# Block 0 of the long filter: folding moved from VectorE into TensorE's accumulation, with a mirrored copy by ScalarE, another order and other buffers for w2

## The chip, the cores and the metric

The kernel runs on one core of one Trainium2 chip. The metric is device time of one execution in microseconds (us). Three runs before the change gave 187.36 to 187.61, median 187.47. A time is compared within the same chip; lower is better.

## The reference

Two branches share the input `q` (2048 rows S, 640 channels D, bf16), and a gate mixes them:

```
x = A_q
g = sigmoid((x * gate_w).sum(-1))                       # one number per row
# branch A: a long convolution over the 2048 rows, per channel
kv = (4-tap causal filter of k) * v
y  = irfft(rfft(pad(kv)) * rfft(pad(ssm_k)))[:2048]     # length 4096
a  = x * (y + kv * ssm_D)
# branch B: an MLP across the rows
h = layernorm(x);  u = gelu(einsum("sd,sf->df", h, w1) + b1)      # F = 1536
b = (einsum("df,fs->ds", u, w2) + b2).T
out = g * a + (1 - g) * b
```

`ssm_k` is the long filter: 640 channels, each with 2048 taps. `ssm_D` enters the kernel as an extra added to tap 0 (row `drow`).

## The kernel before

**The long convolution** is cut into P = 4 blocks of n = 512 rows. Filter block i and signal block j are each turned into frequency space by matmuls with sine and cosine tables (`TFc`, `TFs` for the filter, `AFc`, `AFs` for the signal), multiplied pairwise (`pair`), and turned back (`inverse`). A block is folded first: sample and mirrored sample are added and subtracted, so that the transform needs half as many products. For filter block i this is `w_turn`:

- `wnat{i}` [128, 5 x 512]: the block as it lies in memory, with channels on the partitions (five groups of 128 channels), taps along the free axis. `wnat_load` brings it in one DMA of 640 KB.
- `en{..}`: the folded block. Two VectorE operations over 128 x 1280 add and subtract forward and backward views; four small ones (five columns each, one for each channel group) set the samples that have no mirror image.
- The folded block has to have taps on the partitions. For blocks 0 and 1 TensorE transposes it, 20 matmuls of 128 columns against an identity (`ident`, printed as `idp`) into four PSUM tiles of 640 columns. Blocks 2 and 3 go through a DMA transpose.
- `WEV` says which engine copies each of the four tiles to `eo{i}`: for block 0 ScalarE, VectorE, ScalarE, VectorE; for block 1 four times ScalarE.
- For block 0 the fourth tile also takes `drow`, by two matmuls with one row of the identity.

`w_freq` (tag `wf{i}`) then runs the transform on `eo{i}`, eight tiles of 640 columns in matmuls of 320, evicted by ScalarE to `W{i}` or, for block 1, `Wo`. In the rows of the profile `TFs#2`, `TFc#0` and the like name one of these tiles.

**What else runs in the first 50 us.** ScalarE makes the tables (`Sin`, `Abs`: `TFs`, `adx`, `TFc`, `AFs`, `AFc`) from `idx`, which VectorE makes from `frow`, which GpSimd makes. VectorE takes layer-norm statistics of the 16 row tiles of `q` (`stats`, `mv`) and normalises them to `h`. `shd` and `dg` prepare the 4-tap filter; `cv0`, `cv1` run it on TensorE as 64 x 64 matmuls of `dg` and `kT`, and ScalarE evicts to `ks`. The rows of `v` come partly by plain DMA, partly by GpSimd's indirect gather (`rev` holds the indices). `es0`, `es1` are the folded signal blocks, and TensorE's first MLP matmuls (`m1_0`, on `h` and `w1`) fill in between.

**The second MLP layer** (`mlp2`, tag `m2_q`) takes `w2` in eight pieces of 256 columns, 768 KB each, through three buffers `w2_0`, `w2_1`, `w2_2`; the turn of buffers is (0, 1, 0, 1, 2, 0, 1, 2). A piece is loaded by SP's queue when the buffer's last reader is done. The inverse transforms, the gate (`gg`, `omg`, `c2`) and the products with `q` (`xe`) close the kernel. The very last operations on VectorE are two `fin` operations (scalar_tensor_tensor from PSUM) after the last piece of w2, followed by two stores.

**What sets the order.** Each operation is first gathered in `_Plan` with its engine, reads and writes. `ORDER`, a list of all operation numbers written into the file, says in which sequence they are emitted; each engine works through its own queue in that sequence, and a tracker puts in the semaphore waits. DMAs stand in the queue of SP (plain ones) or GpSimd (gathers, adds to memory), so a DMA that waits for a buffer holds those behind it. PSUM is four tiles `pp` of 128 x 1024 f32, given out in turn, each free again when its eviction is done. Buffers in SBUF lie at written-out offsets (`OFFS`) and share space when their lifetimes are apart; `v1`, for one, lies over `wnat0`.

All matmuls carry line 311 in the profile, ScalarE's activations 695, VectorE's tensor_tensor 657, tensor_scalar 664, copies 672, plain DMAs 265 (262 on GpSimd), gathers 726, the evictions by VectorE 1023.

Of the kernel before, what the change touches and what calls it, by code (L numbers as in the profile page):

```python
# [422 lines left out]
def _checked(items, offs, base, top):  # L423
# [49 lines left out]
def _build(nc, A_q, A_k, A_v, A_shift_k, A_ssm_k, A_ssm_D, B_x, B_w1, B_b1, B_w2, B_b2, gate_w, out):  # L473
# [5 lines left out]
    n = S // P  # L479
# [990 lines left out]
```

## Time and profile before

| | |
|---|---|
| median of three runs | 187.47 us (187.36 to 187.61) |
| the profiled execution | 188.28 us |
| its span, first to last instruction | 186.4 us |
| TensorE busy | 176.8 us (95%), 1578 matmuls |
| VectorE busy | 178.8 us (96%), 252 instructions |
| ScalarE busy | 127.1 us (68%), 205 instructions |
| GpSimd busy | 35.3 us (19%), 68 instructions |
| DMA traffic | 40.37 MB, mean 217 GB/s |

Times in the profile count from the start of the span; 1.88 us of the profiled execution lie outside it. A row of the timeline has start, duration (both us), engine, line, operation, output<-input, shape, and in brackets the idle time of the engine before it and who ended that. A row of the groups has the number of instructions behind an x, then busy us, the mean of one in ns, and the idle time before them. In the table of stretches each engine has its busy time and, behind an x, its instructions, in the order PE, PEld (weight load), DVE (VectorE), ACT (ScalarE), POOL (GpSimd), then granted TensorE clock, busy share of the DMA engines and GB/s. The granted clock is 1.00 throughout.

### The profile page before, as it was taken

The page shows a single profiled execution, that of the slowest core. Times are in us where ns is not written, and L with a number is a line of the kernel's source. Part 1 is how long each engine was busy: PE and PEld are TensorE (multiplying, and loading weights), DVE is VectorE, ACT ScalarE, POOL GpSimd, SP SyncE. Part 2 cuts the span into 40 slices and gives each one's busy share as a digit, 9 for nine tenths or more (in the row PEclk, how much of TensorE's full clock was granted, in tenths as well). Part 3 has the DMA queues.
Part 4 walks back from the last instruction along what each step waited for, and adds up shares of the span by engine and source line. Part 5 has one row for each costly group of instructions (what it writes and reads, how often), then busy time and mean ns, then how long its engine had stood idle before and what let it go on. Part 6 is the DMA issues. An engine that isn't in the chain of part 4 may idle for free.

```text
span 186.4 us, 3923 instructions
## 1 busy us (share of the span) xinstructions
PE 176.8 (95%) x1578; PEld 122.0 (65%) x1578; DVE 178.8 (96%) x252; ACT 127.1 (68%) x205; POOL 35.3 (19%) x68
## 2 busy tenths in 40 slices
PE   7778899999999999999999999999999999999992
PEld 2255667566667766777777777677776777777771
DVE  7999999999999999999899999999999999999784
ACT  3979899879499579638830146644889555875870
POOL 8367067610000000011000000000000500350262
PEclk9999999999999999999999999999999999999999
DMA  5999999798995998598769999988999998999394
GB/s 148 344 311 242 168 184 232 212 212 211 240 333 120 221 234 195 117 224 219 161 143 175 270 252 211 216 156 263 282 270 294 281 190 242 320 182 234 72 136 146
DMA packets 80448, 40.37 MB, mean 217 GB/s; under 512 B 39400, under 2 KB 80238, under 8 KB 80430
## 3 DMA queue, kind: packets, MB, share of 16 engines
q1 hardware_dynamic: 77694, 37.18, 80.9%
q0 software_dynamic: 2736, 2.95, 10.2%
q8 instruction: 12, 0.20, 0.5%
q14 instruction: 6, 0.05, 0.1%
HBM read 26.03 MB, written 7.54 MB: 180 GB/s over the span
## 4 chain that ended last, share of the span: by engine, by line
PE 64%; DVE 23%; DMA 6%; issue 2%; POOL 2%; ACT 1%; DVEq 0%; POOLq 0%
PE pp L311 64%; DVE stats L931 6%; DMA w<-in_B_w_dram 6%; DVE v L657 3%; DVE en L657 3%; DVE es L657 2%; DVE idx L664 2%; DVE W L657 2%; POOL rstd L936 1%; DVE h L665 1%; DVE eo L1023 1%; DVE mv L933 1%; DVE A L657 1%; DVE xe L657 1%; DVE dg L1012 1%
## 5 line engine op out<-in xcount | busy, mean ns | idle before, releaser
L311 PE MATMUL pp<-h,w 128*128 128x320 bf16 x384 | 56.6, 299 | 0.2
L311 PE MATMUL pp<-gT,w 128*128 128x320 bf16 x336 | 48.7, 299 | 0.6 <-DMA w<-in_B_w_dram 0.5
L311 PEld LDWEIGHTS pp<-h,w 128*128 128x128 bf16 x384 | 36.8, 98 | 15.9 <-issue 1.6
L311 PEld LDWEIGHTS pp<-gT,w 128*128 128x128 bf16 x336 | 32.5, 98 | 13.9 <-DMA w<-in_B_w_dram 1.1
L657 DVE TENSOR_TENSOR tt<-A,W 128x3840 bf16<-128x3840 bf16 (+2 forms) x16 | 27.8, 1738 | 0.2
L695 ACT ACTIVATE A<-pp 128x640 bf16<-128x640 f32 x32 | 21.3, 703 | 8.1 <-PE pp L311 8.1
L657 DVE TENSOR_TENSOR Z<-Z,tt 128x3840 bf16<-128x3840 bf16 (+1 forms) x14 | 26.1, 1867 | 0.1
L262 POOL DMA_DIRECT2D out_dram<-xe x3 | 4.1, 1367 | 66.4 <-DVE y L657 57.5
L695 ACT ACTIVATE pq<-pp 128x640 bf16<-128x640 f32 x16 | 11.0, 703 | 7.2 <-PE pp L311 7.1
L695 ACT ACTIVATE gT<-pp,bf 128x640 bf16<-128x640 f32 x12 | 9.5, 791 | 7.9 <-PE pp L311 7.9
L695 ACT ACTIVATE o<-pp,c,omg 128x640 bf16<-128x640 f32 x13 | 11.5, 881 | 4.6 <-PE pp L311 4.6
L931 DVE BATCH_NORM_STATS2 stats<-x 128x6 f32<-128x320 bf16 x32 | 13.7, 473 | 0.0
L695 ACT ACTIVATE xe<-xe,gg 128x640 bf16<-128x640 bf16 x16 | 12.8, 827 | 0.9 <-DMA xe<-rows_q 0.8
L695 ACT ACTIVATE ks<-pp 128x512 bf16<-128x512 f32 (+1 forms) x24 | 11.3, 523 | 3.1 <-PE pp L311 3.1
L657 DVE TENSOR_TENSOR Z<-A,W 128x3840 bf16<-128x3840 bf16 x6 | 12.8, 2153 | 0.5 <-PE pp L311 0.5
L695 ACT ACTIVATE W<-pp 128x640 bf16<-128x640 f32 x18 | 12.1, 720 | 1.5 <-PE pp L311 1.5
L675 POOL MEMSET W<- 1x640 bf16 x4 | 2.7, 665 | 51.1 <-ACT nq L695 49.8
L657 DVE TENSOR_TENSOR W<-W 128x2560 bf16<-128x2560 bf16 x8 | 11.9, 1486 | 0.2
L311 PE MATMUL pp<-kT,dg 64*64 64x256 bf16 x320 | 10.2, 270 | 0.3 <-ACT Wo L695 0.3
L657 DVE TENSOR_TENSOR Z<-Z 128x1280 bf16<-128x1280 bf16 (+1 forms) x16 | 10.0, 653 | 0.1
L311 PE MATMUL pp<-eo,TFc 128*128 128x320 bf16 x48 | 8.9, 300 | 1.2 <-ACT TFc L695 1.2
L262 POOL DMA_DIRECT2D out_dram<-rows_o x6 | 7.0, 1355 | 15.3 <-DMA out_dram<-o 13.2
(156 smaller groups left out, 305.1 us busy)
## 6 DMA issues: line engine op xcount, KB each, us to landing
w<-in_B_w_dram SPq DMA_DIRECT2D x24, 256.0 KB, 4.5
w<-in_B_w_dram SPq DMA_DIRECT2D x8, 768.0 KB, 6.2
wnat<-in_A_ssm_k_dram SPq DMA_DIRECT2D x4, 640.0 KB, 5.2
x<-in_A_q_dram SPq DMA_DIRECT2D x7, 320.0 KB, 6.5
out_dram<-o SPq DMA_DIRECT2D x6, 320.0 KB, 5.4
v<-in_A_v_dram SPq DMA_DIRECT2D x4, 320.0 KB, 3.9
rows_q<-in_A_q_dram SPq DMA_DIRECT2D x8, 160.0 KB, 3.5
xe<-rows_q SPq DMA_DIRECT2D x8, 160.0 KB, 6.1
```

Source lines behind the costliest of these rows:

```text
L262: ins = engobj.dma_start(out_ap, in_ap, accum_op=ALU.add)
L311: ins = self.nc.tensor.matmul(ps_ap, lhsT=lhsT, rhs=rhs, start=start, stop=stop)
L657: return vop(eng, c, lambda e: e.tensor_tensor(out_, in0, in1, op), [in0, in1], [out_], pr, kind="tt")
L664: return e.tensor_scalar(out_, in0, s1, None, op0=op0)
L665: return e.tensor_scalar(out_, in0, s1, s2, op0=op0, op1=op1)
L675: return vop(eng, 0.03 + nel(ap) / 1200.0, lambda e: e.memset(ap, val), [], [ap], pr, kind="ms")
L695: return e.activation(out_, src, func, **kw)
L931: vop("DVE", 0.393, (lambda o_, i_: lambda e: e.bn_stats(o_, i_))(o_, i_), [i_], [o_], pr, kind="bn")
L933: vop("DVE", 0.11, (lambda o_, i_: lambda e: e.bn_aggr(o_, i_))(o_, i_), [i_], [o_], pr, kind="ba")
L936: vop("POOL", 0.7, (lambda o_, i_, e_: lambda e: e.tensor_tensor(o_, i_, e_, ALU.pow))(b["rstd"][:, sl], b["vpe"][:, sl], bc(c_mh, [[8, 12 ...
L1012: vop("DVE", 1.45, lambda e: e.tensor_tensor(o_, ib, sb, ALU.mult), [i_, s_ap], [o_], 1.8, kind="tt")
L1023: vop("DVE", 0.74, lambda e: e.tensor_copy(dst, src()), [src], [dst], 0.3, ps=[p_], kind="ev")
```

## The change

For block 0 alone (`PF = (0,)`) `w_turn` calls a new function, `pf_turn`.

- `wnat0` comes in two DMAs of 320 KB, first and second half of the taps, each half of a channel group stored 257 elements apart (`GAP`) so that one free column stands behind every half.
- Five small VectorE operations (five or ten columns) form `sd0` and write the samples that have no mirror image into `wnat0` itself, so that every forward and backward run of 128 columns is regular.
- One ScalarE copy, `wr`, writes both mirrored halves (128 x 1280) backwards.
- TensorE folds: for each 128 columns one matmul with `wnat0` against `ident` and one with `wr` against `ident` or against its negative (`idn`) are accumulated in the same PSUM place. 40 matmuls of 128 columns in place of 20. `drow` is added with `two`, a row holding 2, and the evictions scale partition 0 by a half (`cst` column 7).
- The six `en` operations of block 0 and the memset of `wnat0`'s margin go. GpSimd gets two more memsets of `cst`, two of `two`, and the making of `idn`.
- The w2 pieces take buffers in the turn (0, 1, 0, 2, 1, 0, 2, 1).
- `ORDER` is another list. In it the first operations stand as before (VectorE's up to its 22nd, ScalarE's up to its third `Abs`). ScalarE then runs `AFs`, the table `TFc` and block 1's evictions in another mixture, `wr` after the third `Wo` eviction of block 1, and block 0's two evictions spread among the remaining `Wo`. TensorE runs block 1's transposes, six of its eight transform tiles, then block 0's transposing groups, the one with `drow` first, with transform tiles between them, and one group behind the three tiles of `cv0`. GpSimd's first gather of `v0` stands right behind the last memset of `TFs`; the gathers of `v1` stand later. In SP's queue the `v0` load stands before the first transpose to `kt0`; piece 3 and piece 4 of w2 are asked for in the new turn, and two loads of `v2` stand behind piece 2's.

```diff
+    PF = (0,)
...
+        buf("idn", [128, 128], BF16, 0, 30)
+        buf("wr", [128, 2, DC, 128], BF16, 0, 30)
+        buf("two", [1, 128], BF16, 0, 30)
+        for i in PF:
+            buf(f"sd{i}", [128, 2, DC], F32, 0, 30)
...
+        memset(cst[:, 7:8], 1.0, 0.2)
+        memset(cst[0:1, 7:8], 0.5, 0.2)
+        memset(b["two"][:, :], 0.0, 0.3)
+        memset(b["two"][:, 0:1], 2.0, 0.3)
...
+        ts(b["idn"][:, :], b["id_i"][:, :], 0.0, -1.0, ALU.is_equal, ALU.mult, 0.25, eng="POOL")
...
+        GAP = n // 2 + 1
+        RT = DC * GAP
+        def pf_turn(i):
+            plan.tag = f"wt{i}"
+            wn = b[f"wnat{i}"]
+            eo = b[f"eo{i % 2}"]
+            for hf in range(2):
+                dst = bass.AP(tensor=wn, offset=hf * RT, ap=[[DC * n + 16, 128], [GAP, DC], [1, n // 2]])
+                dma(dst, dram(A_ssm_k, i * n + hf * (n // 2), [[S, 128], [128 * S, DC], [1, n // 2]]), f"wnat{i}_{hf}", -300.0)
+            pr = 1.0 + 0.1 * i
+            def at(v, extra=None):
+                return bass.AP(tensor=wn, offset=v, ap=[[DC * n + 16, 128]] + (extra or []) + [[GAP, DC]])
+            sd = b[f"sd{i}"]
+            tt(sd[:, 0, :], at(RT + 128), at(128), ALU.subtract, pr)
+            tt(sd[:, 1, :], at(RT + 128), at(128), ALU.add, pr)
+            tt(at(GAP - 1), at(RT), sd[:, 0, :], ALU.subtract, pr)
+            tt(at(RT + GAP - 1), sd[:, 1, :], at(0), ALU.subtract, pr)
+            io = at(RT, [[-RT, 2]])
+            tt(io, io, sd[:, :, :], ALU.add, pr)
+            wr = b["wr"]
+            act(wr[:, :, :, :], bass.AP(tensor=wn, offset=GAP - 1, ap=[[DC * n + 16, 128], [RT, 2], [GAP, DC], [-1, 128]]), ACT.Copy, pr)
+            for e in range(2):
+                for k in range(2):
+                    p_ = _PS()
+                    xd = i == 0 and e == 1 and k == 1
+                    mms = []
+                    for c in range(DC):
+                        f0 = c * GAP + (0 if k else RT)
+                        fw = bass.AP(tensor=wn, offset=f0, ap=[[DC * n + 16, 128], [1, 128]])
+                        bw = wr[:, k, c, :]
+                        mms.append((p_, c * 128, 128, fw, ident, not xd or c in (0, 4), False))
+                        mms.append((p_, c * 128, 128, bw, b["idn"][:, :] if e else ident, False, not xd))
+                    if xd:
+                        mms += [(p_, c0, cn, b["two"][:, :], b["drow"][:, c0:c0 + cn], False, True)
+                                for c0, cn in ((0, 512), (512, 128))]
+                    pe([p_], mms, pr, cost=0.56 + (0.35 if xd else 0.0))
+                    evict(WEV[i][2 * e + k], eo[:, e, k, :], p_, cst[:, 7:8])
...
         def w_turn(i):
+            if i in PF:
+                return pf_turn(i)
...
-            nm = f"w2_{(0, 1, 0, 1, 2, 0, 1, 2)[q]}"
+            nm = f"w2_{(0, 1, 0, 2, 1, 0, 2, 1)[q]}"
...
```

`evict` takes the scale as a new argument: on ScalarE as the activation's scale, on VectorE as a tensor_scalar multiplication in place of the plain copy. The new list of `ORDER` is left out above.

More of the change, by code (lines that the diff above doesn't have):

```diff
@@ L1016, in _build @@
         WEV = (("ACT", "DVE", "ACT", "DVE"), ("ACT", "ACT", "ACT", "ACT"))
-        def evict(eng, dst, p_):
-            if eng == "ACT":
+        GAP = n // 2 + 1
[35 more added lines that the diff above has]
+                    evict(WEV[i][2 * e + k], eo[:, e, k, :], p_, cst[:, 7:8])
@@ L1020, in evict @@
+        def evict(eng, dst, p_, sc=None):
+            if sc is not None and eng == "ACT":
+                act(dst, flat(p_), ACT.Copy, 0.3, scale=sc, ps=[p_])
+            elif sc is not None:
+                src = flat(p_)
+                vop("DVE", 0.74, lambda e: e.tensor_scalar(dst, src(), sc, None, op0=ALU.mult), [src, sc], [dst], 0.3, ps=[p_], kind="ev")
+            elif eng == "ACT":
                 act(dst, flat(p_), ACT.Copy, 0.3, ps=[p_])
@@ L1237, in mlp2 @@
             w2_load(q)
-            w2 = b[f"w2_{(0, 1, 0, 1, 2, 0, 1, 2)[q]}"]
+            w2 = b[f"w2_{(0, 1, 0, 2, 1, 0, 2, 1)[q]}"]
             o_ = b[f"o{(q // 2) % NO}"]
```

75 rows, old and new, of tables (OFFS, ORDER) are left out of this document.

## The prediction

> **What bounds the kernel now.** I read the page's head and its chain first, then the busy time of each engine in stretches, then the chain in order of time, then the instructions of the first 50 us.
>
> ```profile
> span 186.4 us, 3923 instructions
> PE 176.8 (95%) x1578; PEld 122.0 (65%) x1578; DVE 178.8 (96%) x252; ACT 127.1 (68%) x205; POOL 35.3 (19%) x68
> PE 64%; DVE 23%; DMA 6%; issue 2%; POOL 2%; ACT 1%; DVEq 0%; POOLq 0%
> ```
>
> TensorE and VectorE are both full over the span, so the question is which of them binds where. The stretches below (us, then PE, PEld, DVE, ACT and POOL busy) are cut at the first depthwise-convolution matmul of block 0 (20.47), at the last wait for VectorE (49.76) and at the one wait for a w2 piece (143.57).
>
> ```profile
> 8.24:20.47 12.23, 9.61 (x86) 6.21 (x87) 12.23 (x38) 10.66 (x19) 6.58 (x8) 1.00 1.15 281
> 20.47:49.76 29.29, 28.56 (x323) 19.04 (x324) 29.16 (x70) 25.27 (x45) 10.26 (x13) 1.00 0.94 202
> 49.76:143.57 93.81, 93.23 (x867) 66.73 (x867) 92.74 (x76) 59.89 (x103) 1.24 (x2) 1.00 0.92 218
> 143.57:182.90 39.33, 39.31 (x288) 27.98 (x288) 37.06 (x50) 25.88 (x34) 11.54 (x11) 1.00 0.91 207
> ```
>
> TensorE is idle for 12.23 - 9.61 = 2.62 us in the first stretch, 0.73 in the second, 0.58 in the third, 0.02 in the last. From 20.47 on TensorE is the bound almost everywhere; VectorE shapes only the first 50 us. So the change is paid in TensorE time and can gain only what it takes out of these 3.95 us, plus a little at the tail.
>
> ```profile
> 1.05 0.15 POOL cst L675 x4
> 1.25 0.60 POOL frow L797 x2
> 1.87 2.21 DVE idx L664 x4
> ...
> 12.66 1.48 DVE en L657 x2
> ...
> 14.27 0.09 DVE en L672
> 14.36 0.15 DVE en L657 x2
> ...
> 15.89 0.09 DVE en L672
> ...
> 17.67 0.72 DVE eo L1023
> ...
> 49.76 67.37 PE pp L311 x644
> ...
> 133.21 10.31 DMA w<-in_B_w_dram
> 143.57 36.61 PE pp L311 x268
> ```
>
> These pieces of the chain (start, us, what) hold what the change touches: block 0's fold on VectorE, its two evictions there, and the load of w2 that TensorE waits for.
>
> **VectorE, part by part.** Six `en` operations of block 0 go: 1.48 + 0.09 + 0.15 + 0.09 = 1.81 us. Five five-column operations on `sd0` and `wnat0` come; at 0.15 / 2 = 0.075 each that is 0.38. They depend on one another, but statistics of LN stand between most of them, which hides the latency; with that cover gone each would cost its full duration, some 0.1 more. The two evictions stay and get a scale operand; a plain one takes 0.72 here and I keep that. VectorE comes out 1.4 us ahead, minus 0.1: two more GpSimd memsets stand ahead of the second `frow` (0.15 / 4 = 0.04 each), which releases `idx` and with it the whole start.
>
> **TensorE.** Block 0's transposes go from 20 to 40 matmuls of 128 columns.
>
> ```profile
> 12.05 0.99 PE L311 MATMUL pp<-eo,TFc 128*128 128x320 bf16 x6 [1.18 <-ACT TFc L695]
> 14.51 0.71 PE L311 MATMUL pp<-eo,TFc 128*128 128x320 bf16 x4
> 15.66 0.44 PE L311 MATMUL pp<-idp,en 128*128 128x128 bf16 x5
> 16.03 0.44 PE L311 MATMUL pp<-drow,idp 1*128 1x512 bf16 x2
> 18.45 0.73 PE L311 MATMUL pp<-idp,en 128*128 128x128 bf16 x10 [0.52 <-DVE eo L1023]
> 19.70 0.45 PE L311 MATMUL pp<-idp,en 128*128 128x128 bf16 x5 [0.52 <-ACT eo L695]
> 20.47 0.74 PE L311 MATMUL pp<-kT,dg 64*64 64x256 bf16 x20 [0.32 <-ACT Wo L695]
> ```
>
> Five take 0.44 and ten 0.73, so one more costs (0.73 - 0.44) / 5 = 0.058, each with its own weights; twenty cost 1.1 us. A 320-column matmul takes (0.71 - 0.30) / 3 = 0.137, 0.30 being the drain of a last one. [...]
>
> **ScalarE**, which decides when these matmuls can run:
>
> ```profile
> 8.73 1.99 ACT L695 ACTIVATE eo<-pp 128x640 bf16<-128x640 f32 x3
> 11.26 0.73 ACT L695 ACTIVATE TFc<-adx,cst 128x512 bf16<-128x512 f32 x1
> 11.88 0.73 ACT L695 ACTIVATE AFs<-idx,cst 128x512 bf16<-128x512 int32 x1
> 13.62 3.09 ACT L695 ACTIVATE Wo<-pp 128x640 bf16<-128x640 f32 x5 [1.01 <-PE pp L311]
> ```
> ```profile
> L695 ACT ACTIVATE W<-pp 128x640 bf16<-128x640 f32 x18 | 12.1, 720 | 1.5 <-PE pp L311 1.5
> L695 ACT ACTIVATE W<-pp,cst 128x640 bf16<-128x640 f32 x6 | 4.8, 800 | 0.2 <-PE pp L311 0.2
> L695 ACT ACTIVATE w2r<-w 128x1536 bf16<-128x1536 bf16 x2 | 3.0, 1478 | 0.0
> ```
>
> A back-to-back eviction steps 0.60 ((3.09 - 0.70) / 4), a table 0.62 (11.88 - 11.26). The new backward copy `wr` has 1280 columns; the nearest row is `w2r`, also read backwards, 1478 ns for 1536, so 1478 x 1280 / 1536 = 1.23 us. It cannot be below the 0.72 of a 640-column eviction nor above 1.48. Two evictions gain a scale operand: 0.08 each.
>
> The new order, walked with these steps. ScalarE from 8.73: AFs, `eo1`, TFc, three more `eo1`: 8.73 + 0.62 + 0.60 + 0.62 + 0.60 + 0.60 + 0.70 = 12.5, then `Wo` from 12.7, `shd`, two more `Wo`, and `wr` from 14.6 to 15.8. VectorE, which starts on `sd0` a little before its old 12.66, has prepared `wnat0` by about 14.1, ahead of ScalarE. TensorE begins block 1's transform some 1.2 later than before, but its 1.18 wait for TFc goes; the 28 matmuls that stand ahead of block 0 (28 x 0.137 = 3.8) are covered by ScalarE's steps, and block 0 begins when `wr` is there, at 15.8 + 0.2 = 16.0. Then come 10 small and the two `drow` ones (0.95), 10 small (0.55), 12 and 8 of 320 (1.6 and 1.1), 10 small (0.55): 20.8, when the convolution's first PSUM tile is free. By then it has done ten small and eight 320-column matmuls more than before at 20.47: 0.56 + 1.10 = 1.66 us of work for 0.38 of time. That is 1.28 won by shorter waits, against 1.1 that is added: **0.1 to 0.2 us net in the first stretch**. Bounds: 1.1 lost when no wait shrinks, 2.62 - 1.1 = 1.5 won when all go.
>
> Second stretch. The last ten folded matmuls come after the convolution and end at about 23.9; VectorE's copy of them, its 77th operation, then runs 24.0 to 24.8, and the next transform of block 0 waits 0.7 for it (new). LN's normalisations, queued behind that copy, stay ahead of TensorE's need in my walk. Two short waits of the size of the 0.32 before the convolution come for `es0` and for the Gelu table. So up to some 44 us I get no gain. After that VectorE's lead shows:
>
> ```profile
> PE pp L311 <- DMA w<-in_B_w_dram: 0.5, 1, 0.5
> PE pp L311 <- DVE v L657: 0.3, 1, 0.3
> ```
>
> The wait for `v` at 49.76 and two smaller gaps before it close: **0.4 us**, between 0.73 and a loss of 1.3 (both new waits on the path with nothing won for them).
>
> Third stretch. The wait for w2 piece 3:
>
> ```profile
> 131.44 4.57 SPq L265 DMA_DIRECT2D w<-in_B_w_dram  x2
> 143.57 1.26 PE L311 MATMUL pp<-gT,w 128*128 128x320 bf16 x8 [0.46 <-DMA w<-in_B_w_dram]
> ```
>
> Piece 3 went to buffer 1, which piece 1 leaves only at 133.2, and landed 10.3 us later, behind the `xe` loads and piece 4. Now it goes to buffer 2, free long before, and piece 4 takes buffer 1; TensorE asks for that after piece 2 (48 matmuls, 6.6), 16 of `af3` (2.2), 24 of piece 3 (3.3) and two more: over 12 us against 10.3. **0.5 us won**, between 0 and 0.6. SP's queue moves too: two loads of `v2` now stand behind piece 2's wait for buffer 0, which can hold VectorE up by half a us near 132, where TensorE needs `es2` only at 138.
>
> **The loads and GpSimd.** `wnat0` comes in two pieces with 512-byte runs instead of 1024, and the first gather of `v0` moves forward to about 8.3, right behind the last TFs memset.
>
> ```profile
> DMA packets 606, 0.68 MB, mean 356 GB/s; under 512 B 63, under 2 KB 606, under 8 KB 606
> DMA packets 1274, 0.69 MB, mean 301 GB/s; under 512 B 14, under 2 KB 1273, under 8 KB 1273
> 12.77 2.51 POOL L726 DMA_INDIRECT v<-in_A_v_dram,rev  x1 [0.20 <-issue]
> ```
>
> The first row is the stretch 9.6 to 11.5, in which the old `wnat0` landed, the second 139 to 141.3, where 512-byte runs of w2 came in. For 640 KB (0.655 MB) that is 1.84 and 2.18 us: 0.3 later, and VectorE, busy with statistics, asks for it at about 12.4, so I count nothing. With that cover gone it costs 0.3, and up to 1.0 if the gather's 320 KB (half of the first time, 0.9) goes ahead of it as well. [...]
>
> **Tail.**
>
> ```profile
> 183.14 1.01 DVE L1358 SCALAR_TENSOR_TENSOR xe<-pp,omg,xe 128x320 bf16<-128x320 f32 x2
> ```
>
> These last two operations start 0.26 after TensorE's end (182.90 less rounding); in the new order the addition of `c2` before them stands earlier, so up to 0.15 goes: **0.1**.
>
> **The sum.** First stretch -0.1, second -0.4, w2 -0.5, start +0.1, tail -0.1: -1.0 us. The span of 186.4 becomes 185.4, the profiled execution's 188.28 becomes 187.3 (1.9 lie outside the span and stay), and the median of 187.47, 0.8 under that execution, becomes **186.5**. The ends of the terms: -1.5 to +1.1, -0.73 to +1.3, -0.6 to 0, 0 to +0.3, -0.15 to 0. All at their ends together is unlikely, since they trade: what is won early makes the later waits longer.
>
> **Rivals.**
>
> *The ring of ScalarE, VectorE and TensorE slips.* ScalarE is busy 10.66 of 12.23 in the first stretch and 25.27 of 29.29 in the second, and `wr` adds 1.2 there. The last folded group, VectorE's copy of it and the next transform of block 0 hang on one another. If ScalarE's steps come 1 us or more later than I summed, no early wait shrinks and the 1.1 of matmuls is paid in full, and 0.3 of the new 0.7 wait: +1.1 + 0.3 - 0.5 + 0.1 = +1.0, **188.5**, slower. It speaks for it that ScalarE's ladder has 1.3 us of slack at most; against it that the six evictions ahead of `wr` need only 0.60 each while 28 matmuls run beside them. Chance 0.31.
>
> *Late `wnat0`.* The 0.3 of the load shows and eats VectorE's lead: -1.0 + 0.3 + 0.4 = -0.3, **187.2**. For it: the gather beside it; against it: 0.5 us of cover. That the other turn of buffers does not do its work, because another load holds piece 4 back, comes to about the same (-1.0 + 0.5 = -0.5, 187.0). Chance 0.14 together.
>
> *VectorE's lead is passed on whole.* The first stretch gives 0.7, the second its 0.7, w2 0.6, start +0.1: -1.9, **185.6**. The 0.52 waits for `eo` and 0.5 for `v` speak for it, the 1.1 of added matmuls against it. Chance 0.10.
>
> **How the numbers follow.** The forecast has 0.45. Its own ends are some 0.5 to either side (the terms' uncertainties, mostly the first stretch's 0.4 and the second's 0.3): 186.0 to 187.1. The 80% range reaches to 185.5 for the third rival and 188.6 for the first. This kernel's runs lie 0.25 apart, and 0.2%, or 0.37 us, is about what can be told from no change: faster is under 187.10, slower over 187.84. Faster takes the forecast, the third rival and nothing of the first: 0.55; same most of the second and the forecast's upper end: 0.14; slower 0.31.
>
> **What the profile after would show.** Right: TensorE busy about 178 (1.16 more), its idle time before 20.5 under 1.5 us, first folded group at about 16.0, `wr` at 1.2 us; the small matmuls' rows at 0.058 a piece; no wait for `w` near 143; the wait for `v` near 49 gone. Wrong: `wr` later than 16.5 or over 1.5 us; a wait over 1 us before a transform of block 0 in the second stretch; a new wait of TensorE on a w2 piece after 145; VectorE idle on `wnat0` before 14.

## The result and the profile after

The changed kernel took 190.04 us in the median of six runs (189.10 to 191.24), the kernel before 187.67 (187.36 to 188.03): a ratio of 1.0109 (95% interval 1.0076 to 1.0142). Six more runs (changed_again, below) gave 1.0145 (1.0108 to 1.0182). Ratios here and below are those on record; they differ a little from the quotient of the two medians (1.0126 here). Medians and ranges take in every run, the ratios leave out the slow ones, over 1.5% above the fastest run of their kernel (one each of w2turn_alone, changed_w1_early, fold_early_warm11 and the kernel before). The prediction was 186.5, in a range up to 188.6: wrong in sign, and the range too narrow.

The profiled execution took 189.92, its span is 188.1. The head of its page, and the shares of its chain by engine and by line:

```profile
span 188.1 us, 3967 instructions
PE 177.5 (94%) x1598; PEld 122.8 (65%) x1598; DVE 177.2 (94%) x251; ACT 128.7 (68%) x206; POOL 34.5 (18%) x72
PE 66%; DVE 12%; ACT 10%; DMA 7%; issue 2%; POOL 1%; POOLq 1%; SPq 0%; DVEq 0%
PE pp L311 66%; DMA w<-in_B_w_dram 4%; DMA wnat<-in_A_ssm_k_dram 4%; ACT W L702 3%; DVE stats L943 3%; DVE en L664 2%; DVE idx L671 2%; ACT h L702 2%; ACT ks L702 1%; DVE v L664 1%; ACT pq L702 1%; ACT A L702 1%; DVE y L664 1%; POOL out_dram L739 1%; DVE dg L1024 1%
```

VectorE's share of the chain has fallen from 23% to 12%: in its place stand ScalarE (10%, before 1%) and two transfers, of w1 and of `wnat2`. (Lines have moved: 702 is what 695 was, 664 what 657 was.) TensorE's rows that begin with a wait, the first row of the convolution (21.16) and the last row of all, from its timeline (start, duration, then idle time and releaser in brackets):

```profile
8.38 0.92 PE L311 MATMUL pp<-idp,en 128*128 128x128 bf16 x10 [1.76 <-DVE en L664]
10.19 0.45 PE L311 MATMUL pp<-idp,en 128*128 128x128 bf16 x5 [0.28 <-ACT eo L702]
11.48 1.30 PE L311 MATMUL pp<-eo,TFs 128*128 128x320 bf16 x8 [0.84 <-ACT eo L702]
16.20 0.22 PE L311 MATMUL pp<-idp,wnat 128*128 128x128 bf16 x1 [0.55 <-DVE dg L1024]
21.16 2.40 PE L311 MATMUL pp<-kT,dg 64*64 64x256 bf16 x80
25.29 0.43 PE L311 MATMUL pp<-eo,TFc 128*128 128x320 bf16 x2 [0.53 <-DVE eo L1076]
36.02 0.30 PE L311 MATMUL pp<-es,AFc 128*128 128x320 bf16 x1 [0.40 <-ACT ks L702]
44.86 0.45 PE L311 MATMUL pp<-h,w 128*128 128x320 bf16 x2 [0.55 <-DMA w<-in_B_w_dram]
45.47 0.43 PE L311 MATMUL pp<-v,AFs 128*128 128x320 bf16 x2 [0.16 <-DVE AFs L672]
115.80 1.26 PE L311 MATMUL pp<-h,w 128*128 128x320 bf16 x8 [0.55 <-DMA w<-in_B_w_dram]
182.60 1.79 PE L311 MATMUL pp<-gT,w 128*128 128x320 bf16 x12
```

The account in TensorE's time: the first real matmul 0.14 later (8.38 for 8.24), 1.1 for twenty more matmuls, and waits of 3.86 from there on. Before, the waits behind 8.24 were 1.18, 0.52, 0.52, 0.32, 0.19, 0.29 and 0.46, together 3.48. So 0.14 + 1.1 + 0.38 = 1.6; TensorE's last row ended at 182.88 and now ends at 182.60 + 1.79 = 184.39, which is 1.5. The last 0.2 of the span's 1.7 is the tail. The early waits did shrink, from 2.54 to 1.67 up to the convolution; what they gave came back as waits for `eo` and `ks`, which the prediction had foreseen, and for two pieces of **w1**, which it had not looked at. This one profile accounts for 1.7 us; the medians lie 2.4 apart.

The row at 16.20 needs care. Its releaser is printed as `dg`, which ended at 16.06, 0.14 before it. But in changed_again (below) `dg` ended at 16.11 and this matmul came only at 17.37. What both profiles share is `wr`: the matmul starts 0.26 us after its end (15.94 and 17.11), and the six further kernels below in this order with the new fold show 0.25 to 0.29. So `wr` released it; `dg` happened to end in between.

The second profile of the changed kernel (label changed_again, span 189.2) shows one thing more. Stretches as in the prediction's table, first of the one profile, then of the other:

```profile
8.40:11.50 3.10, 1.97 (x25) 1.36 (x26) 3.10 (x12) 3.10 (x6) 1.36 (x3) 1.00 1.15 323
11.50:13.60 2.10, 2.10 (x15) 1.16 (x16) 2.06 (x10) 1.81 (x5) 0.00 (x0) 1.00 1.19 335
```
```profile
8.40:11.50 3.10, 1.99 (x25) 1.38 (x26) 3.10 (x12) 3.10 (x6) 1.42 (x3) 1.00 1.16 321
11.50:13.60 2.10, 2.10 (x9) 1.24 (x10) 2.07 (x10) 1.02 (x2) 0.00 (x0) 0.54 1.10 370
13.60:16.20 2.60, 2.60 (x16) 1.65 (x14) 2.60 (x9) 2.33 (x5) 0.72 (x1) 0.71 1.27 233
```

After the same thin stretch (TensorE busy 2.0 of 3.1 us) the granted clock fell to 0.54: nine matmuls in 2.1 us instead of fifteen. Block 0's first folded matmul then came at 17.4 instead of 16.2. The clock is not the whole of the loss, as far as it is listed: of the changed kernel's twelve runs the five with a clock of 0.997 or more took 189.10 to 191.24, all of them above the kernel before.

### The profile page after: what moved, and what is told of

It is laid out like the page before. It is cut to its first block, busy times and chain, and to the rows that moved or that the text cites. A ratio compares the mean times of both kernels' runs of the same rounds, so it can differ in the third digit from the quotient of the medians.

```text
span 188.1 us, 3967 instructions
## 1 busy us (share of the span) xinstructions
PE 177.5 (94%) x1598; PEld 122.8 (65%) x1598; DVE 177.2 (94%) x251; ACT 128.7 (68%) x206; POOL 34.5 (18%) x72
## 4 chain that ended last, share of the span: by engine, by line
PE 66%; DVE 12%; ACT 10%; DMA 7%; issue 2%; POOL 1%; POOLq 1%; SPq 0%; DVEq 0%
PE pp L311 66%; DMA w<-in_B_w_dram 4%; DMA wnat<-in_A_ssm_k_dram 4%; ACT W L702 3%; DVE stats L943 3%; DVE en L664 2%; DVE idx L671 2%; ACT h L702 2%; ACT ks L702 1%; DVE v L664 1%; ACT pq L702 1%; ACT A L702 1%; DVE y L664 1%; POOL out_dram L739 1%; DVE dg L1024 1%
## 5 line engine op out<-in xcount | busy, mean ns | idle before, releaser
L311 PE MATMUL pp<-h,w 128*128 128x320 bf16 x384 | 58.1, 299 | 1.1 <-DMA w<-in_B_w_dram 1.1
L702 ACT ACTIVATE pq<-pp 128x640 bf16<-128x640 f32 x16 | 10.7, 709 | 6.2 <-PE pp L311 6.2
L311 PEld LDWEIGHTS pp<-kT,dg 64*64 64x64 bf16 x320 | 8.2, 105 | 2.0 <-issue 1.3
L311 PE MATMUL pp<-eo,TFs 128*128 128x320 bf16 x48 | 8.2, 299 | 0.8 <-ACT eo L702 0.8
```

The costliest lines, as they stand in the source:

```text
L311: ins = self.nc.tensor.matmul(ps_ap, lhsT=lhsT, rhs=rhs, start=start, stop=stop)
L702: return e.activation(out_, src, func, **kw)
```

## The experiments

Two explanations stood against each other from the start: the fold itself, and the order written with it. Later a third was added, the clock. Each kernel was timed against the kernel before on the same chip; ratios are to that, with 95% intervals. The groups of experiments ran on different chips (median of the kernel before: 188.22, 188.18, 188.63, 188.47 and 188.47), so kernels of different groups are compared by their ratios.

**changed_again.** No edit.

> The changed kernel once more, for a second profile and for its scatter (its six runs lay between 189.10 and 191.24, the kernel before between 187.36 and 188.03). Theory R (the new order's transfers): the time that comes back is in waits for w1 pieces, near 44 us and near 115 us, and they differ from run to run, so the gaps before m1_1 and m1_5 differ between the two profiles by more than 0.3 us while the first 25 us agree within 0.1. Theory F (the fold itself): the loss is in matmuls added (1.1 us) and in the wait for block 0's last eviction near 25 us, equal in both profiles; then the scatter must have another origin.

190.65 (190.26 to 192.41). The waits for w1 are there again, 1.4 together instead of 1.1, but each differs by less than the 0.3 that theory R asked for, and the first 25 us did not agree, since the clock fell. Neither theory had that.

**order_alone, fold_alone, w2turn_alone** take the change apart.

```diff
 order_alone = before
-ORDER (old)                      +ORDER (new), old fold's operations in the new ones' places
-w2 turn (0,1,0,1,2,0,1,2)        +(0,1,0,2,1,0,2,1)
 fold_alone = after
-ORDER (new)                      +ORDER (old), wr ahead of the first Wo, v1's gathers behind block 0's matmuls
-w2 turn (0,1,0,2,1,0,2,1)        +(0,1,0,1,2,0,1,2)
 w2turn_alone = before
-w2 turn (0,1,0,1,2,0,1,2)        +(0,1,0,2,1,0,2,1), loads of pieces 3 and 4 change places
```

> The new order and the new turn of w2 buffers with the old fold of block 0 on VectorE (its six operations where the five new ones stand, 20 transposing matmuls, no wr, none of the added memsets). Theory R: the waits for w1 near 44 and 115 us (0.55 each in the changed kernel's profile) are there without the new fold; VectorE runs 1.4 us behind, so dg and the fold are late near 16 us. I expect 188.0 to 189.0, that is slower than before by 0.5 to 1.3. Theory F: without the 1.1 us of matmuls and the wr copy the new order is no worse than the old one and keeps the gain at w2: 187.0 to 187.5.

> The new fold of block 0 (five small operations, wr, 40 matmuls, scaled evictions, added memsets) in the old order with the old turn of w2 buffers; wr stands ahead of ScalarE's first Wo, the gathers of v1 behind block 0's last matmuls, which read what they overwrite. Theory F: +1.1 of matmuls, +0.15 at the start, the two waits of 0.52 before block 0's small groups remain, so 188.7 to 189.5. Theory R: the matmuls lie partly in those waits, which the old order has anyway, and no w1 wait is new: 187.7 to 188.4.

> The kernel before with only the new turn of w2 buffers; pieces 3 and 4 change places in SP's queue, so piece 3 is loaded where piece 4 was (131.4 us). Both theories: TensorE's wait of 0.46 for w2 at 143.6 goes, 187.0 to 187.2 (-0.5). If the time is taken back by later loads or by the tail, 187.4 to 187.6.

- order_alone: 189.46, ratio **1.0075** (1.0051 to 1.0099).
- fold_alone: 188.01, ratio **0.9993** (0.9974 to 1.0011).
- w2turn_alone: 189.05, ratio **1.0046** (1.0024 to 1.0068).

In the old order the fold makes no difference to the median, and the new order costs without it. Theory F fell in both places; theory R's range held fold_alone, and order_alone lies a little above its range. This does not close the sum: order_alone at 1.0075 stands against 1.0145 for the changed kernel on the same chip (intervals apart) and 1.0109 in its first six runs, so 0.3 to 0.7% come from having both at once. Nor did order_alone show theory R's mechanism. The only profile of it is of its slowest run (191.59); there the clock was 0.50 from 11.5 to 16.2 us, and of TensorE's waits for loads one of 0.72 was for piece 2 of w2 at 136.8, two of 0.20 for w1 at 34.8 and 46.2, and none near 115. TensorE's waits in fold_alone:

```profile
PE pp L311 <- DVE en L664: 1.9, 1, 1.9
PE pp L311 <- ACT TFc L702: 1.2, 1, 1.2
PE pp L311 <- DVE wz L682: 1.1, 1, 1.1
PE pp L311 <- ACT Wo L702: 0.8, 1, 0.8
PE pp L311 <- ACT eo L702: 0.3, 1, 0.3
PE pp L311 <- DVE v L664: 0.3, 1, 0.3
```

No wait for `es`, `w` or VectorE's `eo` is left in it. Its convolution began 1.1 us later than before (21.60 for 20.47), just the added matmuls; two thirds of a microsecond of that was left at 50 us, 0.5 at 133, and nothing after 143. The first half vanished in waits that stood behind it. The rest did not: TensorE wanted piece 3 of w2 at 143.4, 0.3 later than before, and it had landed at 142.5, 1.05 earlier than before, though it was asked for 0.6 later; it took 8.6 us and not 10.3. Why, no run shows. The runs say the same in another way: eight of fold_alone's twelve lie at 188.00 to 188.02, while the kernel before scatters from 187.37 to 189.02 on that chip. Its best runs are 0.6 faster than any of fold_alone; the medians do not differ beyond the interval.

w2turn_alone was the surprise. In its profile the wait of 0.46 for piece 3 is gone, and one of 0.6 stands at 142.9 for piece 4: in the old order TensorE asks for piece 4 *before* piece 3, and piece 4 now has the buffer that comes free at 133. The turn alone moves the wait to another piece. That and a wait of 0.3 for w1 near 107 stand against the forecast gain of 0.5; both theories missed here. In the new order, where the wait at 143 did go, the turn was not priced by itself.

**changed_w1_early, changed_warm20** try the two suspects in the changed kernel. (`NWARM` is the number of warming matmuls: 512 columns each on a constant tile `wz`, results unused, with which TensorE fills the time until its first real work.)

```diff
 changed_w1_early: SP's queue
+w1_2 first half (m1_1), w1_1 second half (m1_5) earlier
 kt0 transpose (36.0) ; v1 ;
-w1_2 first half
 ...  w1_1 first half (100.7) ; [second half now here] ; v2 ; v2 ; xt (gt1) ; w2 piece 1
-w1_1 second half (108.6)
 changed_warm20
-    NWARM = 15
+    NWARM = 20
```

> The changed kernel with two loads moved in SP's queue: the first half of w1 for m1_1 (w1_2, asked for at 40.7 us behind the transposing kt0 load and v1) goes ahead of that kt0 load, and the second half of w1 for m1_5 (w1_1, asked for behind piece 1 of w2 at 108.6) goes right behind the first half at 100.7. Theory R (late w1 loads of the new order): TensorE's waits of 0.55 to 0.8 near 44.9 and 115.8 us go, and the median falls by 0.9 to 1.3, to about +0.5 to +0.9% over the kernel before. Theory C (a lower granted clock in the first 20 us): the scatter stays and the median falls by less than 0.5.

> The changed kernel with 20 warming matmuls instead of 15, which reach to about 7.7 us and shorten TensorE's pause before block 1's transposes from 1.8 us to about 0.8. Theory C: the pause makes the granted clock fall between 11.5 and 17 us in some executions (0.991 over the span in the second profile); with the shorter pause every run shows a clock of 0.995 or more and the median falls by 0.3 to 0.8. Theory R: nothing changes (within 0.2), because ScalarE's steps set those microseconds and the lost time lies later.

changed_w1_early: 190.33, ratio 1.0094 (1.0063 to 1.0125), in two groups: four of its runs at 188.27 to 188.96 (clock 0.998 to 1.0), eight at 190.15 to 191.83 (six of them with a clock of 0.980 to 0.991). The profile is of the best run; TensorE's waits in it:

```profile
PE pp L311 <- ACT eo L702: 1.1, 2, 0.8
PE pp L311 <- DVE wz L682: 1.1, 1, 1.1
PE pp L311 <- DVE dg L1024: 0.5, 1, 0.5
PE pp L311 <- DVE eo L1076: 0.5, 1, 0.5
PE pp L311 <- DVE es L664: 0.2, 1, 0.2
```

Both waits for w1 are gone and TensorE ends at 182.7, 1.7 us earlier than in the changed kernel: theory R holds for these 1.1 us and more in this run, the best; eight of the twelve do not show it, the median gains nothing beyond the intervals, and two of those eight list a clock of 0.997 and 1.0. (The `dg` in the third line is `wr` again, which ended 0.25 before that matmul.) changed_warm20: 190.50, ratio 1.0112 (1.0070 to 1.0154); two of six runs still show 0.988 and 0.991, so the pause before 8.4 us alone does not decide the clock. Its profile has 0.9 of wait for w1 and a new one of 0.6 for `xt` (gt1, a transposing load of `q` for the gate): a further transfer without slack.

**fold_early, fold_early_w2** follow the other lead, the fold in the old order.

```diff
 fold_early = fold_alone
 VectorE: ... stats(11.2)
+sd, sd, wnat, wnat, wnat
 stats, stats, stats
-sd, sd, wnat, wnat, wnat
 ScalarE: AFs ; wr ; Wo ...        (wr can now start at once)
 GpSimd: frow
-cst[7] x2
 frow ... TFs
+cst[7] x2
 fold_early_w2: SP's queue
-xe1 x3
 w2 piece 4, w2 piece 3
+xe1 x3
```

> The new fold in the old order (as fold_alone) with three small moves: VectorE's five operations stand two statistics earlier (11.6 us), so that wr fits ahead of ScalarE's first Wo at 12.7 to 13.9, and the two memsets of cst column 7 stand behind both frow. Theory F' (the new fold pays once wr fills ScalarE's idle stretch of 1.0 us before Wo): TensorE's wait of 0.8 for Wo at 15.6 falls to about 0.2, the start comes 0.15 earlier, and the first 22 us give 0.7; waits that the later time had absorbed (es0 near 37, w2 near 143) take back up to half: 187.2 to 187.7. Rival: all of it comes back in those waits, 187.9 to 188.2 as fold_alone.

> As fold_early, and the three loads of xe1 stand behind piece 3 of w2 in SP's queue instead of ahead of it. If the wait for w2 near 143 is what takes back fold_early's gain, this one is 0.3 to 0.6 faster than fold_early; if not, the two are equal within 0.2.

fold_early: **187.45**, ratio **0.9959** (0.9937 to 0.9982), faster than before, as forecast. TensorE's first real matmul is back at 8.28, the wait for `Wo` is gone and the convolution begins at 20.46, where it began before the change, with 1.1 us more work done. That part of the mechanism came as forecast. The gain over the kernel before did not arise there: at 37 us TensorE is 0.1 ahead of it, at 133 0.25, at 142.69 (143.57 before) 0.9. Pieces 2 and 3 of w2 landed 1.1 and 1.6 us earlier, asked for at the same times within 0.1 (5.2 and 8.8 us for 6.2 and 10.3). Why these loads took less is not shown. The best runs, 187.16 and 187.37 before, lie only 0.2 apart. fold_early_w2: 195.37, ratio 1.0378 (1.0331 to 1.0425), a miss. Its ScalarE row tells why:

```profile
141.91 0.83 ACT L702 ACTIVATE xe<-xe,gg 128x640 bf16<-128x640 bf16 x1 [5.48 <-DMA xe<-rows_q]
```

ScalarE's in-order queue held evictions behind an operation that waited 5.48 us for `xe1`, and TensorE waited 2.8 for an `A` and 1.4 for an `o` eviction. The granted clock was 0.74 from 140 to 150 us there, and 0.973 to 0.981 in all six runs, so waits and clock both have a part in the 7.9 us over fold_early; how much each has is not shown. The loads looked idle; what stood behind their reader did not.

**changed_w1_filled, fold_early_half, fold_early_warm11** test the clock and price the matmuls.

```diff
 changed_w1_filled = changed_w1_early
-    NWARM = 15
+    NWARM = 20
+    pe([p_], [(p_, 0, 512, wz, wzb, True, True)] * 3, ...)   # own PSUM tile, ahead of block 1's transform
 fold_early_half = fold_early
-    mms.append((p_, c * 128, 128, bw, b["idn"][:, :] if e else ident, False, not xd))
 fold_early_warm11 = fold_early
-    NWARM = 15
+    NWARM = 11
```

> changed_w1_early with 20 warming matmuls instead of 15 and with three more of them (0.64 us, results unused) in TensorE's pause of 0.84 us before block 1's transform. Theory C2: TensorE was busy only 1.97 of the 3.1 us from 8.4 to 11.5 (2.4 to 2.5 in the stable kernels), and that thin stretch lets the granted clock fall afterwards in some executions; filled, all runs show a clock of 0.995 or more and lie like changed_w1_early's good ones, 188.2 to 189.0. Rival: the two groups of runs (188.3 to 189.0 and 190.2 to 191.8) come from elsewhere, transfers for instance; the spread stays and the clock still falls in some runs.

> fold_early without the 20 matmuls that add wr (the mirrored half is left out of block 0's fold; wr is still made). It prices the added matmuls by themselves. If they lie on the path they give 1.1: 186.2 to 186.5. If later waits take back the time, as they did for fold_alone, the gain is 0.2 to 0.6: 186.9 to 187.3.

> fold_early, the steadiest kernel so far (all its runs at a clock of 0.998 to 1.0), with 11 warming matmuls instead of 15: TensorE's pause before block 1's transposes grows from 1.4 to 2.3 us or more, and nothing else changes. Theory C2: less TensorE work in the first 12 us makes the clock fall in some executions (under 0.995) and those cost 0.5 to 1.5 us. Rival: no run shows a lower clock, and the time stays within 0.2 of fold_early (187.5).

fold_early_half: 187.62, ratio 0.9962 (0.9940 to 0.9985). Twenty matmuls fewer give **nothing** that the intervals of 0.2% can tell (fold_early: 0.9959). Both expectations had a gain in them. Its profile, of its slowest run (188.31), has what fold_early's has not:

```profile
PE pp L311 <- DMA w<-in_B_w_dram: 1.0, 2, 0.7
PE pp L311 <- ACT Wo L702: 0.6, 2, 0.3
```

An earlier TensorE waits for pieces 2 and 3 of w2. Here too the loads themselves were slower: piece 3 took 10.9 us, for 8.8 in fold_early's profile. fold_early_warm11: 189.06, ratio 1.0018 (0.9984 to 1.0052), 0.6% or 1.1 us over fold_early by the ratios and 1.4 over fold_early_half on the same chip, and eleven of twelve runs with a clock of 0.978 to 0.991, where none of fold_early's or fold_early_half's is under 0.998. So four warming matmuls fewer, in a kernel that is otherwise steady, do make the clock fall, and it costs time: the seven runs at 0.978 to 0.982 took 188.31 to 190.30, the four at 0.989 to 0.991 took 187.33 to 189.51. In the stretch from 11.5 to 13.6 us the clock reads 0.54 in changed_again, 0.50 in order_alone and 1.00 in the changed kernel's first profile: it differs from one execution of the same kernel to the next. By what rule it falls, and for how long, no run shows.

changed_w1_filled: 191.02, ratio 1.0145 (1.0109 to 1.0181), was inconclusive. No clock is under 0.996, but its filler had to wait for a PSUM tile and came at 11.4 instead of 10.6; it delayed block 0 by 0.5, and the profile has 0.9 of wait for `xt`, pushed back by the moved w1 load. Its stretch from 8.4 to 11.5 was as thin as the changed kernel's (2.05 of 3.1 us), so this stretch by itself does not decide the clock.

**changed_swap, changed_mended** move the loads of w1 without pushing back `xt`, and give TensorE work in its pause.

```diff
 changed_swap = after, SP's queue
 w1_2 first half ahead of kt0 (as changed_w1_early)
 xt (gt1) ;
+w1_1 second half
 w2 piece 1 ;
-w1_1 second half
 changed_mended = changed_swap
-    NWARM = 15
+    NWARM = 20
+    if i == 1 and e == 0 and k == 0:      # spare columns of block 1's last transposing tile
+        mms += [(p_, 640, 384, wz, wz3, True, True)] * 4
```

> The changed kernel with the first half of w1 for m1_1 ahead of the kt0 load (as in changed_w1_early) and the second half of w1 for m1_5 just ahead of piece 1 of w2, behind the gt1 load of xt, which keeps its place. Theory R+C: the late transfers are gone, so a part of the runs lies at 188.2 to 188.9; the others, with slowed matmuls in the first 20 us, lie 1 to 2.5 higher, and show a clock under 0.998 for the most part. Theory R alone: with xt no longer pushed back all runs lie at 188.2 to 189.0.

> changed_swap with 20 warming matmuls instead of 15 and four unused matmuls of 384 columns in the spare columns of the last tile of block 1's transposes, so that they run in TensorE's pause from 10.6 to 11.5 us without a tile of their own (the three of changed_w1_filled had to wait for one and came at 11.4). Theory R+C: the early TensorE work is as dense as in the stable kernels, so no run has slowed matmuls and all lie at 188.1 to 189.0. Theory R alone: the same as changed_swap. If neither, the upper group of runs stays although the early stretch is dense, and its origin is a transfer not found yet.

changed_swap: 190.67, ratio 1.0143 (1.0094 to 1.0192); clock 0.981 to 0.991 in five of six runs, and so less gain than either theory had. The profile (192.45) shows the clock at 0.50 from 11.5 to 13.6 us, none of the waits for w1 or `xt`, and a new one of 1.7 for VectorE's `AFs` at 47.3. changed_mended: 190.44, ratio 1.0116 (1.0084 to 1.0148); clock 0.999 to 1.0 in all six, spread 0.9 instead of 2.5. Its early stretch, and what TensorE waited for longest:

```profile
8.40:11.50 3.10, 2.61 (x30) 1.66 (x30) 3.10 (x12) 3.10 (x6) 1.37 (x3) 1.00 1.16 322
11.50:13.60 2.10, 2.10 (x15) 1.15 (x16) 2.06 (x10) 1.81 (x5) 0.00 (x0) 1.00 1.08 362
```
```profile
PE pp L311 <- DMA w<-in_B_w_dram: 1.5, 1, 1.5
```

With the stretch filled (2.61 of 3.1 busy) the clock is mended, and so is the scatter, but not the median: in the profile 1.5 us of wait for piece 2 of w2 took it. Longer warming and the filling were put in together, so which of them mended the clock is not shown. Piece 2 is asked for when piece 0 leaves the buffer (128.5), and TensorE stands idle for it from 5.15 us later; it took 4.9 us in changed_w1_early's profile and 6.6 here.

**changed_ring, fold_early_ring** give that piece a buffer that is free earlier.

```diff
 changed_ring = changed_mended
-w2 turn (0,1,0,2,1,0,2,1)
+w2 turn (0,1,2,0,1,2,0,1)         piece 2 asked for at 125.5, behind the first v2 load
 fold_early_ring = fold_early
-w2 turn (0,1,0,1,2,0,1,2)
+w2 turn (0,1,2,1,0,2,1,0)         piece 2 asked for at 125, behind v2
```

> changed_mended with the pieces of w2 in the plain turn of buffers (0, 1, 2, 0, 1, 2, 0, 1); piece 2 is asked for at 124.5, right behind the first load of v2, instead of at 128.5 when piece 0 leaves its buffer. In changed_mended TensorE waited 1.5 us for piece 2 near 135. Theory R (late transfers, with the early clock mended): the wait goes and nothing else is left, so all runs lie at 188.2 to 189.2, about the kernel before. If a further transfer waits in its turn, 189.5 to 190.5 with a new wait of TensorE on a DMA in the profile.

> fold_early with the turn of buffers (0, 1, 2, 1, 0, 2, 1, 0), so that piece 2 is asked for at 125 us behind v2 instead of at 126.8 and piece 4 at 131 in buffer 0. Theory R: the scatter of fold_early (187.16 to 188.53) comes from pieces 2 and 3 landing within 1 us of being asked for; with more slack for piece 2 the median falls by 0 to 0.3 and the spread shrinks. Rival: the earlier piece pushes the xe loads behind it and the time rises by 0.2 to 1.

changed_ring: 188.98, ratio 1.0048 (1.0005 to 1.0091). By the ratios 0.7%, or 1.3 us, are back, and the changed kernel, with w1, clock and w2 mended, comes near the kernel before. Four of its runs still lie at 189.8 to 190.5, three of them with a clock of 1.0 and one with 0.990; its profile (188.93) shows 0.6 of wait for `xt` and 0.6 for `es`. fold_early_ring: **187.23**, ratio **0.9938** (0.9902 to 0.9973), the fastest of all; its profile's span is 185.0, 1.4 less than before the change. By how much it beats fold_early (0.2) is inside the intervals, and the spread did not shrink (186.80 to 188.61).

## Why the prediction was wrong

- **Start, +0.1: right.** `idx` starts at 2.03 instead of 1.87, behind the two memsets.
- **Small matmuls, 0.058 each: right.** Within a group of ten they follow one another by 0.05 to 0.07 us in the rows from 16.20 on.
- **`wr` from 14.6 to 15.8, 1.23 us: right** in place and nearly in size, and block 0 did begin when it was there, at 16.20 for 16.0:

```profile
14.65 1.29 ACT L702 ACTIVATE wr<-wnat 128x1280 bf16<-128x1280 bf16 x1
15.81 0.73 ACT L702 ACTIVATE Wo<-pp 128x640 bf16<-128x640 f32 x1
```

- **First stretch, -0.1: mis-sized**, +0.2. Waits gave 0.87 instead of 1.28 against the 1.1 of added matmuls. The convolution began at 21.16 instead of 20.8: 0.2 of it by `wr`, 0.2 because the work between took 4.96 us and not 4.75. Idle time before 20.5, which should have been under 1.5, was 1.8.
- **Second stretch, -0.4: this is the step that failed.** By the rows above the waits in it grew from 0.48 (0.19 and 0.29) to 1.64: +1.2. The waits that the prediction itself had counted as new came, 0.53 for `eo` (forecast 0.7), 0.40 where `es0` is read, and 0.16 for `AFs` where it had expected one for the Gelu table; they were paid in full: the sum had put the time up to 44 us at nothing, without naming what would make up for them. The wait for `v` went. The other 0.55 is a term that the sum did not have. I had walked the engines and the w2 loads, and not the w1 loads in SP's queue. The first load of w1 for m1_1 stands behind the transposing load `kt0`, as it did before the change; the three rows of SP are given for the changed kernel, then for the kernel before with TensorE's first matmuls on that load:

```profile
35.98 4.05 SPq L260 DMA_TRANSPOSE kt<-ks  x1
40.08 0.57 SPq L265 DMA_DIRECT2D v<-in_A_v_dram  x1
40.70 0.46 SPq L265 DMA_DIRECT2D w<-in_B_w_dram  x1
```
```profile
36.09 3.40 SPq L260 DMA_TRANSPOSE kt<-ks  x1
39.54 0.58 SPq L265 DMA_DIRECT2D v<-in_A_v_dram  x1
40.16 1.77 SPq L265 DMA_DIRECT2D w<-in_B_w_dram  x2
44.69 1.79 PE L311 MATMUL pp<-h,w 128*128 128x320 bf16 x12
```

  Now it is asked for at 40.70 and TensorE wants it at 44.31: 3.6 us, for a load that takes 4.1. Before, it was asked for at 40.16, took 3.9 and was used at 44.69, with some 0.6 us to spare. The place in the queue did not change here: `kt0` held SP for 0.65 longer, the load took 0.2 more, and TensorE was there 0.4 sooner. Why `kt0` took longer is not shown.
- **w2, -0.5: right for the wait, wrong for the stretch**, +0.1. The wait at 143 went in the changed kernel. In its place came 0.55 for w1 at 115.8, whose load the new order had put behind piece 1 of w2 in SP's queue (asked for at 108.6 instead of 100.9). And the turn of buffers alone is no gain (w2turn_alone).
- **`wnat0` 0.3 later: wrong.** The second half was there at 10.9, the whole at 11.5 before (the trace has no landing of the first half, which was asked for ahead of it); the 512-byte runs cost nothing that shows.
- **Tail, -0.1: wrong**, +0.1 to 0.2: the chain ends on GpSimd behind its last scatter, where before it ended on the `fin` operations.
- **The clock: not forecast at all.** The page before had 1.00 throughout, and I took that as given for a kernel with another pattern of early pauses. Seven of the changed kernel's twelve runs have 0.978 to 0.991.
- **The rivals.** The slower one had the right sign and the wrong mechanism: ScalarE's steps came on time. That VectorE's lead is passed on whole has no run for it: in fold_early, the fold in the old order, the gain stands at the loads of w2 and not in the first 50 us.

Beneath it lies one error: I priced each edit against the waits of the profile before, and counted a wait that goes as time won. fold_alone and fold_early_half show that here it isn't: 1.1 us of TensorE work, added or taken away before 24 us, moves the median by no more than the intervals can tell (0.2%). The profiles show two reasons: half a microsecond goes into waits behind it, and the later loads of w1 and w2, which arrive just as TensorE gets there, take 1 to 2 us more or less from one profile to the next. What stays open is why those loads vary, why the new order costs 0.3 to 0.7% more with the new fold than with the old one, why changed_ring still has an upper group of runs, and which part of the changed kernel's scatter is clock and which is transfers; a part of the clock's effect is probably not in the records (below).

## What to carry to other kernels

When an order is written anew along with an edit, split the two before pricing either: here the edit alone left the median as it was, the order with its turn of buffers cost 0.75%, and all together 1.1 to 1.45%. List every load with its request, its landing and the time of its first reader, and count as the new bound each one with less between the last two than such loads vary by from one profile to the next (1 to 2 us here); a gain upstream can be paid out only as far as the tightest of them allows (in fold_early_half, with twenty matmuls fewer, TensorE waited 1.0 us for pieces 2 and 3 of w2). And a change that moves TensorE's first pauses can change its clock (with four warming matmuls fewer, 0.978 to 0.991 in eleven of twelve runs, where none of fold_early's was under 0.998), so look at more than one profile.

## What the hardware showed

In fold_early_warm11's profile TensorE's matmuls followed one another at about half the usual pace for some 6 us while the granted clock reads 1.00. Its timeline, and the stretch that holds these rows:

```profile
10.69 1.25 PE L311 MATMUL pp<-eo,TFs 128*128 128x320 bf16 x4
12.61 1.78 PE L311 MATMUL pp<-eo,TFc 128*128 128x320 bf16 x6 [0.67 <-ACT TFc L702]
17.30 0.71 PE L311 MATMUL pp<-eo,TFc 128*128 128x320 bf16 x4
```
```profile
13.60:16.20 2.60, 2.60 (x11) 1.51 (x10) 2.60 (x6) 1.43 (x3) 2.08 (x3) 1.00 1.17 251
```

Four matmuls of 320 columns take 1.25 us at 10.7 and 0.71 at 17.3, eleven in a stretch that holds 27 in fold_early's profile (some of them shorter ones of 128 columns), and no entry of the clock tells it. That it is the same fall of the clock is likely from the pace, and not shown; this run, at 190.08, was the second slowest of the kernel's twelve and is listed with a clock of 0.999. Here the spacing of like matmuls, 1.25 us for 0.71 over four, tells what the listed clock does not. And the time from request to landing of piece 2 of w2 (768 KB) varied from 4.9 to 6.6 us between two profiles with much the same queue ahead of it, changed_w1_early's and changed_mended's; the difference of 1.7 is more than the slack that pieces 2, 3 and 4 had in the profile before (under 0.1, none and 0.4 us).
